# Four loads under way instead of eight in a fused three-block kernel

## The chip, the cores and the metric

The kernel runs on one core of a Trainium2 chip. The metric is the device time of one execution in microseconds (us). All times below come from the runs and from one profiled execution of the kernel.

## What is computed

Three blocks follow each other, all in float32, on 4 batches of 576 positions:

```python
def reference(**kwargs):
    attn_out = _attn_ref(q, k, v)              # (4, 8, 576, 64); heads 0-3 see 32 local keys, 4-7 see keys 32 apart
    x = attn_out.transpose(0, 2, 1, 3).reshape(B, S, H * D)
    x = _moe_ref(x, ...)                       # h = relu(x @ w_in); u * (w_spatial @ norm(v) + b_spatial) @ w_out
    return _moe2_ref(x, ...)                   # 4 experts: causal softmax attention, weighted by a top-2 gate
...
    scores = scale * np.matmul(q, k.transpose(0, 1, 3, 2))     # block 1
    scores = np.where(masks[None, :, :, :], scores, -1000000000.0)
    attn = np.exp(scores - scores.max(-1)); attn /= attn.sum(-1) + 1e-09
    return np.matmul(attn, v)
```

Inputs are q, k, v, and the weights of the two later blocks. Some weights arrive as float64 (`w_in`, `w_out`) and are split into two float32r halves on the chip, so that three matmuls stand for one float32 product (`mm3`, lines 618 to 620).

## The kernel before

**Order.** Nothing waits on a barrier between stages. Each piece of work is a generator (`a1_load`, `a1_scores`, `v_half`, `project`, ...) and a planner, `Plan.run`, picks from their steps one after the other by rank, by planned engine times, and by three tables of numbers (NUDGE, HOLD, LEAN). The order in which it picks is the order in which instructions stand on each engine: on PE, DVE, ACT and POOL, and on SP, which issues nearly all DMAs. Every engine works through its own row in order. Across engines, semaphores hold an instruction until its inputs are there.

**Loads.** All reads of inputs are issued by SP. Lines 796 and 799 load q and k of a pair of heads (288 KB each, `a1_load`), line 818 the values (`a1_load_v`, 48 to 256 KB a piece), line 666 a float64 weight (512 KB, `weight`), line 659 a float32 weight (144 to 288 KB), lines 733, 736 and 743 the tail of `w_spatial`. There are 100 of them, and they stand in places 1 to 100 of SP's row. Behind them on SP come only copies between tiles on the chip (L1362, L1366) and the stores of the result (L1622). The first 50 loads stand close together at the start; the next 50 wait for a buffer or for a stage to end and come in small bunches.

**What already holds a load back.** The framework gives each DMA one of eight semaphores in turn (DMAHW0 to DMAHW7), and a DMA that takes a semaphore again waits until the DMA that had it before has landed. So at most eight are under way.

**Steps that the prediction speaks of.** L1050 are the matmuls of block 1's attention with its values, on 64x64 corners of the array: short, and many. L981 and L983 turn the attention tiles (`a`, which POOL or DVE has just divided by its sums at L914). L844 and L856 are block 1's scores. L531 are matmuls on zeros, put in by `fill` where the planner sees PE idle in the first 46 us. L618 to L620 are dense products. On DVE, L673 is the first step on a float64 weight that has landed, L1062 subtracts the high half of block 1's result (which ACT copied at L639) from PSUM.

```python
        yield "sp", 0.46, [("a1", b)] + prev, dict(c=2)
        qt, kt = C([128, S], F, "q"), C([128, S], F, "k")
        nc.sync.dma_start(qt, qk[b, hp, :, 0, :])
```

Of the kernel before, what the change touches and what calls it, by code (L numbers as in the profile page):

```python
# [14 lines left out]
B, H, S, D = 4, 8, 576, 64  # L15
# [2 lines left out]
NEG = -8.0e9  # L18
NCHUNK = 75
EXPERTS_AHEAD = 4  # L20
TAILS = 3
ALONE = 3
TRANK = 15
# [444 lines left out]
def fused(tc, qk, vl, vw, vs, win, wsb, woutT, wp, wo, out):  # L468
    nc = tc.nc
# [6 lines left out]
    const, chunk, small, psum = [c.__enter__() for c in ctx]  # L476
    plan = Plan(dict(c=NCHUNK, w64=3, bd=TAILS, al=ALONE, eps=8, mx=8, ps=8, sq=PSUM_BANKS["d"] - 1, **PSUM_BANKS))
    plan.within = dict.fromkeys(PSUM_BANKS, "ps")
# [23 lines left out]
    def f(t):  # L502
        return t.bitcast(F)

    act, dve, pool, pe = nc.scalar, nc.vector, nc.gpsimd, nc.tensor


# [43 lines left out]
    m = mloc[:32]  # L551
# [13 lines left out]
    for h in range(2):  # L565
        for m, nr, off in ((mstr, 3, 0), (mstl, 2, 28)):
            m = m[64 * h:64 * h + 64].rearrange("p (c i) -> p c i", i=18)
# [7 lines left out]

    bd = [const.tile([128, 2, 128], R, name=f"bd{i}") for i in range(TAILS)]

# [74 lines left out]
    def weight(keys, src, r0, rows, c0, cols, after=(), summed=False, alone=False):  # L652


        n = len(keys)
        if src.dtype == F:
            yield "sp", 0.46, after, dict(c=1)
            m = C([rows, n * cols], F, "st")
            nc.sync.dma_start(m.rearrange("p (a c) -> p a c", a=n),
                              src[r0:r0 + n * rows, c0:c0 + cols].rearrange("(a p) c -> p a c", a=n))  # L660
            plan.dma(n * rows * cols * 4)
            plan.lat = 0.0
        else:
            yield "sp", 0.46, after, dict(w64=1)
            w = chunk.tile([rows, cols, 2], I32, name=nm("w64"), tag="w64", bufs=3)
            nc.sync.dma_start(w.rearrange("p a b -> p (a b)"),
                              src.bitcast(I32)[r0:r0 + rows, 2 * c0:2 * (c0 + cols)])
            plan.dma(rows * cols * 8)


            yield "dve", 1.75, (), dict(c=2)
            a, p2 = C([rows, cols], I32, "a"), C([rows, cols], I32, "p2")
            dve.tensor_scalar(a, w[:, :, 1], 3, 0x3FFFFFFF, op0=ALU.logical_shift_left, op1=ALU.bitwise_and)  # L673
            dve.scalar_tensor_tensor(a, w[:, :, 1], -0x40000000, a, op0=ALU.bitwise_and, op1=ALU.bitwise_or)
            dve.tensor_scalar(p2, a, -0x800000, None, op0=ALU.bitwise_and)
            if not summed:


                yield *(((("act", "dve"), (t_act(cols), t_fast(cols)))) if alone else hi_of(cols)), (), dict(c=2)
                hi, wl = (C([rows, cols], R, n) for n in ("wh", "wl"))  # L680
                if plan.eng == "act":
                    act.activation(hi, f(a), AF.Copy, scale=1 + 2.0 ** -22)
                else:
                    engine().tensor_scalar_mul(hi, f(a), 1 + 2.0 ** -22)
                yield "dve", 1.65, (), {}
                d = w[:, :, 1]
                dve.tensor_scalar(d, d, 23, None, op0=ALU.logical_shift_left)
                dve.scalar_tensor_tensor(f(a), w[:, :, 0].bitcast(dt.uint32), 2.0 ** -9, d, op0=ALU.mult, op1=ALU.add)
                dve.scalar_tensor_tensor(wl, f(a), 2.0 ** -43, f(p2), op0=ALU.mult, op1=ALU.mult)
                plan.give("w64")  # L690
                plan.give("c", 2)
                key, = keys
                W[key] = (hi, wl)
                plan.set(("W", key))
                return
            yield "dve", t_dve(cols), (), dict(c=1)
            m = C([rows, cols], R, "m")
            engine().scalar_tensor_tensor(m, w[:, :, 0].bitcast(dt.uint32), 2.0 ** -52, f(p2), op0=ALU.mult, op1=ALU.mult)
            plan.give("w64")
            yield *hi_of(cols), (), dict(c=1)  # L700
            hi = C([rows, cols], R, "wh")
            copy(hi, f(a))
            yield "pe", t_mm(cols, 6), (), dict(x=1)
            ps = P([rows, cols], "x")
            pe.matmul(ps, ident, f(a), start=True, stop=False)
            pe.matmul(ps, unit, m, start=False, stop=False)
            pe.matmul(ps, minus, hi, start=False, stop=True)
            plan.give("c", 3)
            yield *out_of(cols), (), dict(c=1)
            wl = C([rows, cols], R, "wl")  # L710
            copy(wl, ps)
            plan.give("x")
            key, = keys
            W[key] = (hi, wl)
            plan.set(("W", key))
            return
        yield *((("act", "dve"), (t_act(n * cols), t_fast(n * cols))) if alone else hi_of(n * cols)), (), dict(c=1)
        hi = C([rows, n * cols], R, "wh")
        copy(hi, m)
        yield *(("dve", t_dve(n * cols)) if alone else lo_of(n * cols)), (), dict(c=1)  # L720
        wl = C([rows, n * cols], R, "wl")
        engine().tensor_sub(wl, m, f(hi))
        plan.give("c")
        for i, key in enumerate(keys):
            W[key] = (hi[:, i * cols:i * cols + cols], wl[:, i * cols:i * cols + cols])
            plan.set(("W", key))

    def spatial_tail():

        n = S - 512  # L730
        yield "sp", 0.46, [("x",0,3,0)], dict(c=2)
        m, mb = C([128, S], F, "st"), C([97, S], F, "mb")
        nc.sync.dma_start(m[:n, :], wsb[512:S, :])
        plan.dma(n * S * 4)
        yield "sp", 0.46, (), {}
        nc.sync.dma_start(m[n:, :], wsb[512:S, :])
        plan.dma(n * S * 4)
        r = plan.ready
        yield "pool", 0.6, (), {}
        pool.memset(mb[64:97, :], 0.0)  # L740
        for row in (64, 96):
            yield "sp", 0.46, (), {}
            nc.sync.dma_start(mb[row:row + 1, :], wsb[S:S + 1, :])
            plan.dma(S * 4)
        plan.ready = max(plan.ready, r)
        yield *hi_of(S), (), dict(c=2)
        hi, wl = C([128, S], R, "wh"), C([97, S], R, "wl")
        copy(hi, m)
        yield *hi_of(S), (), {}
        copy(wl[64:97, :], mb[64:97, :])  # L750
        yield "dve", t_dve(2 * S, 2), (), {}
        dve.tensor_sub(wl[96:97, :], mb[96:97, :], f(wl)[96:97, :])
        dve.tensor_sub(wl[:n, :], m[:n, :], f(hi)[:n, :])
        plan.give("c", 2)
        W["sp", 4] = (hi, wl)
        plan.set(("W", ("sp", 4)))
# [31 lines left out]
    def a1_load(b, hp):  # L788
        local = hp < 2
        order = [(bb, h) for bb in range(B) for h in range(4)]  # L790
        n = order.index((b, hp))
        d = 4
        prev = [("a", *order[n - d], 1)] if n >= d else []
        yield "sp", 0.46, [("a1", b)] + prev, dict(c=2)
        qt, kt = C([128, S], F, "q"), C([128, S], F, "k")
        nc.sync.dma_start(qt, qk[b, hp, :, 0, :])
        plan.dma(128 * S * 4)
        yield "sp", 0.46, (), {}
        nc.sync.dma_start(kt, qk[b, hp, :, 1, :])
        plan.dma(128 * S * 4)  # L800
        r = plan.ready
        plan.set(("ld", b, hp))
        A1[b, hp] = dict(q=qt, k=kt, nk=64 if local else 54, v=[], a={}, x=None)
        plan.set(("qk", b, hp), r - plan.end)

    def a1_load_v(b, hp):
        local = hp < 2
        if wide(b, hp):
            parts = [(96, min(512, 1152 - i), vw[b - 2, hp, :, i:min(i + 512, 1152)]) for i in range(0, 1152, 512)]
        elif local:  # L810

            parts = [(128, 512, vl[b, hp, :, 512 * i:512 * i + 512]) for i in range(2)] + [(64, 256, vl[b, hp, :64, 1024:])]
        else:
            parts = [(128, 128 * (j1 - j0), vs[b, hp - 2, :, 128 * j0:128 * j1]) for j0, j1 in ((0, 2), (2, 6))]
        for i, (rows, cols, src) in enumerate(parts):
            yield "sp", 0.46, [] if i else [("ld", b, hp)], {} if i else dict(c=len(parts))
            t = C([rows, cols], F, "v")
            nc.sync.dma_start(t, src)
            plan.dma(rows * cols * 4)
            A1[b, hp]["v"].append(t)  # L820
        plan.set(("v1", b, hp), plan.ready - plan.end)
# [560 lines left out]
    def ahead(b, e):  # L1382
        n = 4 * b + e - EXPERTS_AHEAD
        return [("edone", *divmod(n, 4))] if n >= 0 else []
# [399 lines left out]
```

## Time and profile before

| | |
|---|---|
| median of 3 runs | 434.56 us (434.14 to 434.62) |
| the profiled execution | 434.02 us |
| its span, first to last instruction | 432.1 us |
| PE busy | 419.5 us, 97% of the span |
| DVE busy | 318.7 us, 74% |
| ACT busy | 267.1 us, 62% |
| POOL busy | 141.1 us, 33% |
| HBM read, written | 26.59 MB, 4.72 MB |

The page of the profile gives busy times, the DMA queues and the costliest groups. Further views of the same trace are used below: the waits (who waited for whom), the chain of work that ended last in order of time, a table by stretches of time, a timeline of one engine, and the DMA queues and issues of one stretch. "PEld" is the loading of PE's weights, which runs beside the matmuls. "Issue" as the cause of a wait means that the engine waited for nothing that the profile shows.

### The profile page before, as it was taken

What the parts mean: (1) busy time and instruction counts of PE and PEld (TensorE: products, weight loads), DVE (VectorE), ACT (ScalarE), POOL (GpSimd) and SP (SyncE); (2) the same over time, 40 slices, a digit from 0 to 9 for tenths busy, and PEclk for the clock granted to TensorE, in tenths of its full rate; (3) what the DMA queues carried; (4) which work ended last, traced back from release to release, by engine and by line L of the source; (5) the groups of instructions that cost most, each with busy time, mean ns of one, the idle gap of its engine ahead of it and who ended that gap; (6) DMA issues with size and microseconds to landing.
All of it is one profiled execution on the core that took longest, in us unless ns stands there. A gap on an engine that the chain in (4) does not pass through costs nothing.

```text
span 432.1 us, 11509 instructions
## 1 busy us (share of the span) xinstructions
PE 419.5 (97%) x4156; PEld 382.7 (89%) x4156; DVE 318.7 (74%) x1189; ACT 267.1 (62%) x827; POOL 141.1 (33%) x258
## 2 busy tenths in 40 slices
PE   7869999999999999999999999999999999999996
PEld 3557899999999889998999899999999999988885
DVE  6998998264577742347979863698888899988872
ACT  3666776154598841224405532887788779779973
POOL 3551876541152340221508911112022005215210
PEclk9999999999999999999999999999999999999999
DMA  7999105121561000334000006805251332162043
GB/s 297 340 361 308 35 2 175 67 79 36 157 205 44 2 2 2 122 101 167 2 1 2 2 0 155 194 1 126 67 134 43 94 79 58 24 160 98 26 148 121
DMA packets 22844, 43.58 MB, mean 101 GB/s; under 512 B 3202, under 2 KB 5634, under 8 KB 22788
## 3 DMA queue, kind: packets, MB, share of 16 engines
q1 hardware_dynamic: 22628, 42.72, 32.9%
q8 instruction: 33, 0.54, 0.5%
q14 instruction: 23, 0.19, 0.1%
q10 hardware_dynamic: 160, 0.13, 0.1%
HBM read 26.59 MB, written 4.72 MB: 72 GB/s over the span
## 4 chain that ended last, share of the span: by engine, by line
PE 95%; DVE 1%; DMA 1%; issue 1%; ACT 1%; POOL 0%; SPq 0%; ACTq 0%
PE pd L618 17%; PE pd L620 17%; PE pd L619 17%; PE pt L1488 4%; PE pd L1206 4%; PE pd L1207 4%; PE pd L1208 4%; PE px L1050 4%; PE ps L856 2%; PE px L1536 2%; PE ps L1401 2%; PE ps L1400 2%; PE px L1534 2%; PE px L1566 2%; PE pt L981 2%; PE pd L1210 1%
## 5 line engine op out<-in xcount | busy, mean ns | idle before, releaser
L1423 POOL TENSOR_SCALAR a<-a,asums 128x256 f32<-128x256 f32 (+3 forms) x23 | 23.1, 1010 | 87.1 <-DVE asums L1431 52.5
L914 POOL TENSOR_TENSOR a<-a,rs 128x216 f32<-128x216 f32 (+5 forms) x32 | 25.3, 797 | 55.2 <-DVE rs L912 26.3
L618 PE MATMUL pd<-xh,wh 128*128 128x288 f32 x128 | 38.8, 303 | 0.0
L1388 DVE CUSTOM_DVE_ANT_0 a<-ps,mqk 128x512 f32<-128x512 f32 (+4 forms) x72 | 33.5, 482 | 7.2 <-PE ps L1401 5.3
L1414 ACT ACTIVATE a<-a,amx 128x384 f32<-128x384 f32 (+3 forms) x64 | 35.6, 557 | 5.0 <-DVE amx L1388 4.9
L1206 PE MATMUL pd<-wh,vh 128*128 128x288 f32 x128 | 38.2, 298 | 0.0
L618 PE MATMUL pd<-gh,fh 128*128 128x288 f32 x128 | 38.1, 297 | 0.0
L619 PE MATMUL pd<-xl,wh 128*128 128x288 f32 x128 | 37.7, 295 | 0.0
L620 PE MATMUL pd<-gh,fl 128*128 128x288 f32 x128 | 37.7, 295 | 0.0
L1207 PE MATMUL pd<-wl,vh 128*128 128x288 f32 x128 | 37.7, 294 | 0.0
L620 PE MATMUL pd<-xh,wl 128*128 128x288 f32 x128 | 37.7, 294 | 0.0
L619 PE MATMUL pd<-gl,fh 128*128 128x288 f32 x128 | 37.7, 294 | 0.0
L1208 PE MATMUL pd<-wh,vlo 128*128 128x288 f32 x128 | 37.7, 294 | 0.0
L1121 DVE BATCH_NORM_STATS2 bst<-vr 128x6 f32<-128x512 f32 x18 | 12.4, 691 | 25.2 <-ACT vr L645 25.2
L1477 DVE TENSOR_TENSOR e<-pt,e 128x384 fp32r<-128x384 f32 (+1 forms) x48 | 27.6, 598 | 3.7 <-ACT e L639 3.2
L645 ACT ACTIVATE vr<-pd 128x512 f32<-128x512 f32 x17 | 10.1, 594 | 30.5 <-PE pd L620 29.0
L1214 DVE TENSOR_TENSOR u<-pd,u 128x288 f32<-128x288 f32 x32 | 13.9, 454 | 18.7 <-PE pd L1211 18.6
L1127 POOL TENSOR_TENSOR rstd<-rstd,neghalf 128x1 f32<-128x1 f32 x18 | 11.9, 664 | 47.4 <-DVE rstd L1125 38.7
L879 ACT ACTIVATE a<-a,mx 128x64 f32<-128x64 f32 (+1 forms) x72 | 24.9, 350 | 3.5 <-DVE mx L870 3.5
L618 PE MATMUL pd<-wh,xh 128*128 128x512 f32 x64 | 26.0, 406 | 0.0
L620 PE MATMUL pd<-wh,xl 128*128 128x512 f32 x64 | 25.1, 392 | 0.0
L619 PE MATMUL pd<-wl,xh 128*128 128x512 f32 x64 | 25.1, 392 | 0.0
(243 smaller groups left out, 1478.3 us busy)
## 6 DMA issues: line engine op xcount, KB each, us to landing
qk<-qk SPq DMA_DIRECT2D x64, 144.0 KB, 2.4
q<-in_qk_dram SPq DMA_DIRECT2D x16, 288.0 KB, 5.2
k<-in_qk_dram SPq DMA_DIRECT2D x16, 288.0 KB, 5.3
w<-in_win_dram SPq DMA_DIRECT2D x8, 512.0 KB, 6.3
out_dram<-o SPq DMA_DIRECT2D x16, 256.0 KB, 2.1
v<-in_vl_dram SPq DMA_DIRECT2D x8, 256.0 KB, 5.9
v<-in_vs_dram SPq DMA_DIRECT2D x8, 256.0 KB, 4.4
w<-in_woutT_dram SPq DMA_DIRECT2D x4, 512.0 KB, 4.4
```

The source lines that it names most:

```text
L618: pe.matmul(ps, ah, bh, start=i == 0, stop=False)
L619: pe.matmul(ps, ah, bl, start=False, stop=False)
L620: pe.matmul(ps, al, bh, start=False, stop=i == n - 1)
L879: act.activation(a[:, c], a[:, c], AF.Exp, bias=mx[:, c:c + 1], scale=-1.0, accum_out=sums[:, c, :1])
L914: engine().tensor_mul(x, x, rs[:, :n].unsqueeze(2).broadcast_to([128, n, nk]))
L1206: pe.matmul(ps, vh[:, fs], wh[:, c0:c0 + cn], start=(i == 0), stop=False)
L1207: pe.matmul(ps, vh[:, fs], wl[:, c0:c0 + cn], start=False, stop=False)
L1208: pe.matmul(ps, vlo[:, fs], wh[:, c0:c0 + cn], start=False, stop=False)
L1388: dve.tensor_tensor_reduce(a[:, s0:s0 + sn], ps, mask, op0=ALU.add, op1=ALU.min, scale=-0.125, scalar=m if s0 else 3.0e38, accum_out=m)
L1414: act.activation(a, a, AF.Exp, bias=m, scale=-1.0, accum_out=st["sums", e][:, i:i + 1])
L1423: engine().tensor_scalar_mul(a, a, r)
L1477: dve.tensor_sub(el, ps, f(eh))
```

## The change

Each load is issued through a small function `load`, which adds a dependency on the load four places ahead of it. The first four are free, and the second bound (200) is never reached by 100 loads.

```diff
+QUEUED = 4
+THROTTLED = 200
...
+    loads = []
+
+    def load(dst, src):
+        i = nc.sync.dma_start(dst, src)
+        if QUEUED <= len(loads) < THROTTLED:
+            tc.add_manual_dep(getattr(i, "ins", i), loads[-QUEUED].name,
+                              mybir.DependencyInfo(mybir.DependencyClass.Sync, mybir.DependencyReason.DATA),
+                              reason="few loads at a time")
+        loads.append(getattr(i, "ins", i))
...
-            nc.sync.dma_start(m.rearrange("p (a c) -> p a c", a=n),
+            load(m.rearrange("p (a c) -> p a c", a=n),
...
-            nc.sync.dma_start(w.rearrange("p a b -> p (a b)"),
+            load(w.rearrange("p a b -> p (a b)"),
...
-        nc.sync.dma_start(qt, qk[b, hp, :, 0, :])
+        load(qt, qk[b, hp, :, 0, :])
```

The other five loads (k, the values, the four of `spatial_tail`) are changed in the same way. The planner knows nothing of it: the rows of PE, DVE, ACT and POOL are the same instructions in the same order with the same waits, and SP has the same 202 instructions in the same order.

What differs is which semaphore a load waits for. SP's row of the kernel before at the start of the program (w is a float64 weight, q and k are a pair of heads, v their values):

```order
L666 DMA w645_159<-in_win_dram 128x1024
L666 DMA w646_161<-in_win_dram 128x1024
L796 DMA q7_163<-in_qk_dram 128x576
L799 DMA k8_164<-in_qk_dram 128x576
L796 DMA q9_167<-in_qk_dram 128x576
L799 DMA k10_168<-in_qk_dram 128x576 [waits DMAHW0_49]
L818 DMA v11_171<-in_vl_dram 128x512 [waits DMAHW1_49]
L818 DMA v12_173<-in_vl_dram 128x512 [waits DMAHW2_49]
```

Here the ninth load, k10, is the first that waits, for the first load (DMAHW0). The same places of SP in the changed kernel:

```order
L510 DMA w645_159<-in_win_dram 128x1024
L510 DMA w646_161<-in_win_dram 128x1024 [waits DMAHW0_49]
L510 DMA q7_163<-in_qk_dram 128x576 [waits DMAHW1_49]
L510 DMA k8_164<-in_qk_dram 128x576 [waits DMAHW2_49]
L510 DMA q9_167<-in_qk_dram 128x576 [waits DMAHW3_49]
L510 DMA k10_168<-in_qk_dram 128x576 [waits DMAHW4_49]
L510 DMA v11_171<-in_vl_dram 128x512 [waits DMAHW5_49]
L510 DMA v12_173<-in_vl_dram 128x512 [waits DMAHW6_49]
```

Now the fifth load waits for the first, and each later one for the load four places ahead: no instruction is added, each wait names a semaphore four places nearer.

## Rows read from the trace of the kernel before

**Rows 1.** The page: span, busy time by engine, the DMA queues (packets, MB, share).

```profile
span 432.1 us, 11509 instructions
...
PE 419.5 (97%) x4156; PEld 382.7 (89%) x4156; DVE 318.7 (74%) x1189; ACT 267.1 (62%) x827; POOL 141.1 (33%) x258
...
q8 instruction: 33, 0.54, 0.5%
```

**Rows 2.** Waits of PE, whole run: us in total, times, longest us.

```profile
PE px L1050 <- issue: 2.6, 2, 1.9
PE ps L844 <- DMA k<-in_qk_dram: 2.0, 1, 2.0
...
PE pt L981 <- issue: 1.4, 1, 1.4
```

**Rows 3.** The chain that ended last, 16 to 40 us: start us, us, what.

```profile
22.88 1.92 issue
...
28.91 1.36 issue
...
36.27 0.72 issue
```

**Rows 4.** By stretches: us, busy (count) of PE, PEld, DVE, ACT, POOL, clock, DMA, GB/s.

```profile
19.40:24.79 5.39, 3.48 (x126) 3.12 (x126) 5.25 (x34) 3.68 (x10) 3.27 (x6) 1.00 1.02 378
24.79:30.26 5.47, 4.11 (x125) 3.08 (x125) 4.75 (x14) 2.86 (x10) 2.29 (x7) 1.00 1.02 361
30.26:36.99 6.73, 6.00 (x127) 4.47 (x127) 6.20 (x13) 2.67 (x6) 1.88 (x5) 1.00 0.88 306
36.99:47.07 10.08, 10.07 (x124) 7.60 (x127) 8.94 (x53) 8.30 (x35) 5.65 (x15) 1.00 0.72 226
```

**Rows 5.** DMA queues in 0.1 us from 22.4, 27.7 and 47.9 us.

```profile
q8 instruction: 1, 0.02, 50.0%
...
q8 instruction: 1, 0.02, 70.3%
...
q8 instruction: 1, 0.02, 75.4%
```

**Rows 6.** DMA issues near 30.5, 74 and 113 us: KB each, us to landing.

```profile
w<-in_win_dram SPq DMA_DIRECT2D x1, 512.0 KB, 7.1
...
k<-in_qk_dram SPq DMA_DIRECT2D x1, 288.0 KB, 4.2
...
k<-in_qk_dram SPq DMA_DIRECT2D x1, 288.0 KB, 2.8
```

**Rows 7.** Timelines of POOL and PE: start us, us, engine line op [idle before].

```profile
27.61 0.82 POOL L914 TENSOR_TENSOR a<-a,rs 128x378 f32<-128x378 f32 x1 [3.76 <-DVE rs L912]
...
28.58 0.32 PE L981 MATMUL pt<-ident,a 128*118 128x128 f32 x1
...
63.28 1.33 POOL L914 TENSOR_TENSOR a<-a,rs 128x216 f32<-128x216 f32 x2 [0.51 <-DVE rs L909]
...
64.55 0.55 PE L981 MATMUL pt<-ident,a 128*118 128x128 f32 x3
```

**Rows 8.** Timeline of DVE: the same columns.

```profile
26.66 0.49 DVE L1062 TENSOR_TENSOR xl<-px,xh 128x320 fp32r<-128x320 f32 x1 [0.59 <-ACT xh L639]
...
37.78 0.64 DVE L1062 TENSOR_TENSOR xl<-px,xh 128x108 fp32r<-128x108 f32 x2 [1.16 <-ACT xh L639]
...
40.95 0.41 DVE L673 TENSOR_SCALAR a<-w 128x512 int32<-128x512 int32 x1
```

**Rows 9.** Waits of DVE from 8.8 to 73.2 us: total, times, longest.

```profile
DVE xl L1062 <- ACT xh L639: 1.7, 2, 1.2
```

**Rows 10.** By stage, columns as in rows 4.

```profile
22.90:37.00 14.10, 10.11 (x253) 7.55 (x253) 12.80 (x30) 6.98 (x20) 5.11 (x13) 1.00 0.96 340
37.00:73.20 36.20, 36.20 (x570) 31.77 (x570) 34.19 (x149) 28.72 (x101) 24.76 (x38) 1.00 0.31 95
73.20:174.00 100.80, 100.80 (x1194) 92.35 (x1193) 54.80 (x290) 55.72 (x236) 34.38 (x62) 1.00 0.24 72
```

More of the change, by code (lines that the diff above doesn't have):

```diff
@@ L732, in spatial_tail @@
         m, mb = C([128, S], F, "st"), C([97, S], F, "mb")
-        nc.sync.dma_start(m[:n, :], wsb[512:S, :])
+        load(m[:n, :], wsb[512:S, :])
         plan.dma(n * S * 4)
         yield "sp", 0.46, (), {}
-        nc.sync.dma_start(m[n:, :], wsb[512:S, :])
+        load(m[n:, :], wsb[512:S, :])
         plan.dma(n * S * 4)
@@ L742, in spatial_tail @@
             yield "sp", 0.46, (), {}
-            nc.sync.dma_start(mb[row:row + 1, :], wsb[S:S + 1, :])
+            load(mb[row:row + 1, :], wsb[S:S + 1, :])
             plan.dma(S * 4)
@@ L795, in a1_load @@
         qt, kt = C([128, S], F, "q"), C([128, S], F, "k")
-        nc.sync.dma_start(qt, qk[b, hp, :, 0, :])
+        load(qt, qk[b, hp, :, 0, :])
         plan.dma(128 * S * 4)
         yield "sp", 0.46, (), {}
-        nc.sync.dma_start(kt, qk[b, hp, :, 1, :])
+        load(kt, qk[b, hp, :, 1, :])
         plan.dma(128 * S * 4)
@@ L817, in a1_load_v @@
             t = C([rows, cols], F, "v")
-            nc.sync.dma_start(t, src)
+            load(t, src)
             plan.dma(rows * cols * 4)
```

## The prediction

> **What bounds the kernel now.** I read the page first: PE is busy 419.5 of 432.1 us [rows 1], so the end can only move if PE's idle time changes, or if something makes PE wait. The waits of PE say where that idle time lies. Two of the lines shown have no cause in the kernel at all: 2.6 and 1.4 us, 4.0 in three waits, are put down to "issue" [rows 2]. The one wait for a load is the first of all, 2.0 us for the first k; nothing that the change touches stands ahead of it. After that no load ever ends a wait of PE.
>
> The chain in order of time places the three: 1.92 us from 22.88, 1.36 from 28.91, 0.72 from 36.27 [rows 3]. All lie in the first 46 us, when the loads run. The table by stretches shows what they are. From the end of one wait to the end of the next PE has executed 125 to 127 matmuls and as many weight loads [rows 4], so about 256 instructions; and queue q8, named "instruction", moved 33 packets of together 0.54 MB [rows 1], 16 KB each, which is 8312 PE instructions in pieces of about 252. So PE stands still at the border of a piece of program that has not come yet. A packet of that queue begins at 22.4 and one at 27.7 us [rows 5], each 2.4 to 2.6 us before PE goes on (24.80, 30.27).
>
> How long does such a fetch take? PE crosses a border at 19.4, at 24.80 and at 30.27 (the starts of the stretches in rows 4), and the next piece's packet begins at 22.4 and 27.7: **3.0 and 2.9 us after the border**. After the border at 47.07, when the loads are done, it begins at 47.9: **0.8 us after** [rows 4, 5]. So about 2.1 us of each early fetch are spent waiting while the loads have the DMA engines (DMA share 1.02 in both stretches, rows 4). A load waits there too: one issued near 30.5 lands after 7.1 us, one issued into empty queues after 2.8 [rows 6].
>
> **The change, part by part.** No instruction is added or moved on any engine; 96 waits on SP now name a load four places back, where 92 named one eight back. Behind a waiting load stand only other loads: the 100 loads fill SP's first places, so copies and stores are not held.
>
> *Fetches.* With three other loads ahead of it, a load finds little queued. Four loads of 288 KB at the observed rates (about 350 GB/s, rows 4, 10) take 3.4 us, of which 2.8 is the time of one load alone; so about 0.5 us of waiting is left, where 7.1 less some 3.4 (a 512 KB load alone, my estimate from 2.8 plus 224 KB at 350 GB/s) leave 3.7 now. If a fetch's wait shrinks like a load's, it falls from 2.1 to 0.3 us; bounds are 0 (the row at 47.9) and 2.1 (unchanged). I take 0.5. A fetch from border to execution is then 0.8 + 0.5 + 2.5 = 3.8 us, against 5.4, 5.5 and 6.7 now. PE's own work in the three pieces is 3.48, 4.11 and 6.00 us [rows 4]. What remains of the waits is 0.3, 0 and 0: **3.7 of 4.0 us leave PE's idle time.**
>
> The Trainium skill says, in "Runtime: NRT & Kernel Launch", section "Instruction fetch mechanics", that instructions come in blocks of 16 KiB over a queue of the sequencer's own and that crossing a border is mostly hidden. The trace agrees on the blocks (256 instructions apart) and not on the hiding: three borders cost 4.0 us. By the page there would be nothing to gain here, and the time would stay at 434.6 us.
>
> *What is late next.* PE gets earlier only as far as its inputs do. The first 1.6 us are mostly lost at once: the transpose at 28.58 reads a tile that POOL ends at 27.61 + 0.82 = 28.43 [rows 7], and POOL waited for DVE. DVE in turn had stood still 0.59 us before 26.66 for ACT's copy of PE's late result [rows 8]; only that comes back. So PE gains 0.59 + 0.15 = 0.7 there, then the whole second wait (its fetch now starts earlier and the border comes no earlier than 28.2) and the third: 0.7 + 1.36 + 0.72 = 2.8 us at 37.
>
> From there DVE decides. Between 8.8 and 73.2 us the waits of DVE over 0.3 us are two, 1.7 us together, both for ACT's copy behind a late PE result [rows 9]: 0.59 and 1.16 [rows 8]. Otherwise it works through, 34.19 of 36.20 us in the stage from 37 on [rows 10]. So it can get 1.75 us ahead and no more until 73. PE reads DVE's and POOL's tiles with little in hand: the transposes from 64.55 to 65.10 read tiles of which POOL ends the last at 63.28 + 1.33 = 64.61, some 0.2 us before its use [rows 7]. So of the 2.8 us about **1.75 + 0.2 = 1.95** are left at 65. After 73 PE is busy without a gap (100.80 of 100.80, rows 10) and the other engines have time to spare, so the 1.95 us stay to the end.
>
> *The loads themselves.* A load can only come later. Alone it lands 2.8 us after its issue, so four under way could carry 4 x 288 KB in 2.8 us, 420 GB/s, more than the 340 to 378 that flow now [rows 4, 10]; in a bunch of six with four under way, one took 4.2 [rows 6], which would be 280 GB/s. I take about 3.2 us (370 GB/s), nearer the first row, since loads now start one by one as others land, and not in a burst as there. Then the stream is as fast as now, or up to 1 us late at 37. Nothing waits for it: the weight issued near 30.5 lands by 38.0 and DVE comes to it at 40.95 [rows 6, 8], 2.9 us later, or 1.2 with DVE 1.75 us ahead. Later loads come into queues that are a quarter used (DMA share 0.24, rows 10). Cost: zero, covered by that margin; if it is gone, DVE waits.
>
> *Sum.* On the profiled execution: 434.0 - 1.95 = 432.1. Its median of runs is 0.5 higher, so **432.6 us**; with the fetch wait between 0 and 1 us and the loss to DVE between nothing and 0.8, 431.8 to 433.5.
>
> **The rivals.**
>
> *A part of it, 433.9.* The fetch's wait falls only to 1.5 us (T = 4.8). The first border is passed at 24.2, the second at 29.0, 1.3 us earlier than now, and the third wait goes; of that DVE passes on about half, or late loads eat it: 0.3 to 1.1 us gained, 433.5 to 434.3.
>
> *No change, 434.6.* The fetch does not wait behind the queue of loads but for its turn on a busy engine. The load queue is never empty with four under way either, so the turn comes as late as now: the three waits stay at 1.92, 1.36 and 0.72, and loads come early enough, 434.3 to 434.9. For it: the fetch's extra 2.1 us is less than a load's extra 3.7. Against it: the extra 2.1 us are more than twice what a whole load takes of the engines (288 KB at 350 GB/s, 0.8 us), so it is more than one turn. The Trainium skill has this rule in "DMA: Bandwidth & Descriptors", section "Queues, rings and completion order": each DMA engine takes turns between queues, a packet at a time. The trace speaks against it as the only delay, by the 2.9 to 3.0 us from border to packet, but no run here shows the turns.
>
> *Slower, 438.* Four under way don't fill the DMA engines: at 280 GB/s (the 4.2 us row) what now flows from 8.8 to 37 us (28.2 us at some 350 GB/s, 9.9 MB) takes 35.3 us, 7.1 more. The weight issued near 30.5 then lands near 45 at the latest, where DVE wanted it at 40.95, and DVE stands up to 4 us; it has no gap to take that back before 73, and PE has some 0.2 us in hand [rows 7], so the end comes 3 to 3.9 us later, 437.6 to 438.5, even with the fetches repaired. It decides from about 3 us of delay (38.0 to 40.95), a rate under 9.9 MB / 31.2 us = 317 GB/s.
>
> **How the numbers follow.** A measurement of this kernel tells 0.2%, 0.9 us, from no change. Chances: the forecast 0.62, a part of it 0.14, no change 0.14, slower 0.10. The range leaves out the slower case and the far ends: 431.7 to 434.9. Faster by over 0.2% (under 433.7): the forecast and half of the part, 0.68; within 0.2%: the rest of the part, no change and a little of the slower case, 0.22; slower by over 0.2%: 0.10. The likeliest case's own range is 431.8 to 433.5.
>
> **What would show it.** In the profile after, the "issue" waits of PE should be at most 0.5 us in total, with instruction packets beginning within 1.5 us of each border. A 288 KB load should land some 3 us after issue in the first 40 us (now up to 7). DVE's two waits for ACT's copy should be gone, and a new wait of PE for POOL or DVE should stand near 28 us, another between 41 and 65. Wrong would be: "issue" waits of the same length (no change), a DVE wait for a weight load near 40 us or GB/s under 317 in the first stretches (slower), or PE gaining more than 2.3 us (then DVE was not the limit until 73).

## The result and the profile after

The changed kernel takes **440.57 us** (median, 438.30 to 441.15) beside 434.35 us of the kernel before on the same chip: a ratio of 1.0136, 95% interval 1.0097 to 1.0175. It is slower by 6.2 us, outside the predicted range. The profiled execution is the shortest of its runs, 438.3 us with a span of 436.5 us, 4.4 us more than the span before [rows 1]. One execution of a kernel below (444.19 us, without weights to wait for) was in a slower state of the chip and is left out. The new lines shift the numbering: L1050 of before is L1062 here, L981 is L993, L914 is L926, L673 is L685, L639 is L651, and all loads of the change stand at L510.

The waits of PE, whole run (us in total, times, longest), beside [rows 2]:

```profile
PE pt L993 <- POOL a L926: 3.2, 3, 2.0
PE px L1062 <- ACT aT L651: 2.3, 1, 2.3
...
PE px L1062 <- DVE xl L1074: 1.1, 1, 1.1
PE ps L868 <- DVE rs L924: 0.7, 1, 0.7
```

The three "issue" waits, 4.0 us before, are gone altogether; the forecast had 3.7 of them go. In their place PE waits for POOL, ACT and DVE. What those waited for stands in the waits of DVE (8.8 to 73.2 us, beside [rows 9]) and in two lines of those of ACT (37 to 60 us):

```profile
DVE a L685 <- DMA w<-in_win_dram: 6.9, 4, 3.2
```

```profile
ACT wh L694 <- DVE a L686: 2.4, 1, 2.4
ACT wh L651 <- DMA st<-in_wsb_dram: 1.4, 1, 1.4
```

So both engines end up waiting for loads. DVE stands 6.9 us for float64 weights (w), where it stood for none in this stretch before. ACT stands 1.4 us for a float32 weight (st). The page's chain of work that ended last has PE for 87% of the span and DMA for 6%; before it was 95% and 1%:

```profile
PE 87%; DMA 6%; DVE 5%; ACT 1%; issue 0%; DVEq 0%; SPq 0%
```

In order of time (start, length, what) it runs through four loads between 16 and 62 us:

```profile
19.40 4.99 DMA w<-in_win_dram
...
28.93 5.38 DMA w<-in_win_dram
...
42.51 4.21 DMA k<-in_qk_dram
...
46.78 5.30 DMA st<-in_wsb_dram
...
52.10 0.68 ACT wh L651
52.78 0.28 ACT aT L651
...
53.11 1.30 PE px L1062 x70
```

The last rows are worth following. ACT's row of work has "wh" (a conversion of the weight st) right ahead of "aT", the copy that PE's products at 53.11 need. The weight lands at 52.08, so ACT stands, and PE stands 2.30 us behind it. Before, the same conversion began at 47.59 and did not wait, because its weight had landed at 43.09.

The table by stages shows the stream of loads itself (time, busy and count of PE, PEld, DVE, ACT, POOL, granted clock, DMA share, GB/s), beside [rows 10]:

```profile
8.80:22.90 14.10, 12.88 (x296) 8.41 (x295) 13.72 (x104) 10.52 (x48) 7.03 (x17) 0.93 0.86 266
22.90:37.00 14.10, 11.01 (x242) 8.22 (x236) 10.31 (x25) 6.53 (x20) 4.55 (x12) 0.88 0.82 259
37.00:48.00 11.00, 10.33 (x155) 7.83 (x150) 7.56 (x46) 7.23 (x33) 3.11 (x8) 1.00 0.83 256
48.00:60.00 12.00, 9.70 (x177) 8.54 (x166) 11.32 (x54) 8.81 (x32) 9.93 (x19) 0.86 0.52 155
```

It moves 259 GB/s from 22.9 to 37 us, where 340 flowed before [rows 10]. A single load is faster than it was (the weights of 512 KB in the chain land after 4.99 and 5.38 us, where one needed 7.1 [rows 6]), but too few are under way. From 37 to 60 us the loads are still coming; before, the first 50 were done at 46.3 us. DVE's busy time from 22.9 to 37 falls from 12.80 to 10.31 us.

The sum of the change on the page: PE is busy 422.1 us (419.5 before), and idle for 14.4 (12.6 before):

```profile
PE 422.1 (97%) x4156; PEld 384.6 (88%) x4156; DVE 317.5 (73%) x1189; ACT 267.2 (61%) x827; POOL 140.9 (32%) x258
```

The idle time is 4.0 us less in instruction waits and some 5.8 more in others. The busy time grows where the granted clock falls to half, 1.2 instead of 2.4 GHz. It does so after two of PE's new waits, of 1.98 us from 26.24 and 2.30 us from 50.81 (and once earlier in this execution, from 7.4 to 10.8 us, mostly over matmuls of zeros; the scores behind them begin at 11.54 us, in the kernel before at 11.72):

```profile
28.20:31.20 3.00, 2.98 (x10) 2.54 (x11) 2.93 (x6) 0.73 (x2) 2.60 (x8) 0.50 0.75 217
55.20:58.60 3.40, 3.40 (x15) 3.08 (x13) 3.30 (x10) 3.10 (x14) 1.96 (x4) 0.50 0.09 31
```

Not every wait of about that length is followed by half clock: in the kernel before, 1.92 us at 22.88 was not [rows 3, 4].

What each part costs can be read from the times at which PE comes to the same instructions. Two groups of the same work, before and then after (start, length, what):

```profile
50.11 1.30 PE L1050 MATMUL px<-aT,v 64*64 64x32 f32 x70
...
60.02 1.35 PE L1050 MATMUL px<-aT,v 64*64 64x32 f32 x72
```

```profile
53.11 1.30 PE L1062 MATMUL px<-aT,v 64*64 64x32 f32 x70 [2.30 <-ACT aT L651]
...
64.54 1.35 PE L1062 MATMUL px<-aT,v 64*64 64x32 f32 x72
```

At the border behind which the first instruction wait stood (24.80 before, 22.17 now) PE is 2.6 us ahead of the kernel before, and at 40.05 still 0.26. At 42.20, behind a wait for DVE, it is 0.57 late, and at 53.11, behind the wait for "aT", 3.00. From there it waits for nothing, but at 64.54 it is 4.52 late: the difference comes with the stretch at half clock, 55.2 to 58.6, and stays (4.49 at PE's last matmul). So of the 4.4 us in this execution some 3.0 are what the waits behind late loads cost beyond what the fetches gave, and 1.5 are the clock's. The median is 2 us above this execution, and no trace says where those stand.

This leaves four questions. What do four loads carry, and why less than I took? Is it the weights that cost, or any load? Can the loss by the clock be taken away? And was the gain, the instruction waits, worth what the forecast said?

### The profile page after: what moved, and what is told of

Same layout as the page of the kernel before. It is cut to its first block, busy times and chain, and to the rows that moved or that the text cites. A ratio compares the mean times of both kernels' runs of the same rounds, so it can differ in the third digit from the quotient of the medians.

```text
span 436.5 us, 11508 instructions
## 1 busy us (share of the span) xinstructions
PE 422.1 (97%) x4156; PEld 384.6 (88%) x4156; DVE 317.5 (73%) x1189; ACT 267.2 (61%) x827; POOL 140.9 (32%) x258
## 3 DMA queue, kind: packets, MB, share of 16 engines
HBM read 26.59 MB, written 4.72 MB: 72 GB/s over the span
## 4 chain that ended last, share of the span: by engine, by line
PE 87%; DMA 6%; DVE 5%; ACT 1%; issue 0%; DVEq 0%; SPq 0%
PE pd L630 16%; PE pd L631 16%; PE pd L632 16%; PE pt L1500 4%; PE pd L1218 4%; PE pd L1219 4%; PE pd L1220 4%; DMA w<-in_win_dram 3%; PE px L1062 3%; PE px L1548 2%; PE ps L1413 2%; PE ps L1412 2%; PE px L1546 2%; PE ps L868 2%; PE px L1578 2%; DMA st<-in_wsb_dram 1%
## 5 line engine op out<-in xcount | busy, mean ns | idle before, releaser
L926 POOL TENSOR_TENSOR a<-a,rs 128x216 f32<-128x216 f32 (+5 forms) x32 | 25.4, 798 | 58.8 <-DVE rs L924 30.4
```

The lines of the kernel that those rows point to most:

```text
L926: engine().tensor_mul(x, x, rs[:, :n].unsqueeze(2).broadcast_to([128, n, nk]))
```

## Experiments: how much a number of loads carries

**Loads alone, pieces of 288 KB.** No work but loads; each phase starts when the one before has landed.

```python
PHASES = [(1, 8, 0), (2, 16, 0), (3, 24, 0), (4, 24, 0), (5, 24, 0), (6, 24, 0), (8, 24, 0), (4, 24, 1), (8, 24, 1)]  # under way, loads, matmuls beside
...
            for k in range(n):
...
                i = nc.sync.dma_start(t, qk[k // 8, (k // 2) % 4, :, k % 2, :])
...
                for back in (range(1, 9) if k == 0 else (depth,) if k >= depth else ()):
                    if back <= len(loads):
                        tc.add_manual_dep(i, loads[-back].name, info(), reason="few loads at a time")
```

> This kernel computes nothing of the reference: it only loads 288 KB blocks of q and k, in groups with 1, 2, 3, 4, 5, 6 and 8 loads under way, then with 4 and with 8 while PE works through 500 short matmuls, and stores zeros. Theory A (a load's own way is long, about 4 us once others are under way, and four do not fill the engines): with four, 288 KB land every 0.95 us or slower (310 GB/s or less) also without any PE work, with eight every 0.71 us. Theory B (four fill the engines, but each instruction fetch or other traffic holds up one of the 16 engines, and with four under way the next load waits for that slowest one): four alone reach 390 GB/s or more, within 5% of eight, and only the group beside PE falls to about 300.

Measured, in the steady part of the phases with 2, 3, 4, 5, 6 and 8 under way, then four beside short matmuls (columns: time, PE, PEld, DVE, POOL, clock, DMA share, GB/s):

```profile
30.00:44.00 14.00, 0.00 (x0) 0.00 (x0) 0.00 (x0) 0.00 (x0) 1.00 0.68 210
54.00:72.70 18.70, 0.00 (x0) 0.00 (x0) 0.00 (x0) 0.00 (x0) 1.00 0.82 260
82.00:96.90 14.90, 0.00 (x0) 0.00 (x0) 0.00 (x0) 0.00 (x0) 1.00 0.92 307
108.00:120.70 12.70, 0.00 (x0) 0.00 (x0) 0.00 (x0) 0.00 (x0) 1.00 0.96 326
131.00:141.60 10.60, 0.00 (x0) 0.00 (x0) 0.00 (x0) 0.00 (x0) 1.00 1.01 379
153.00:161.70 8.70, 0.00 (x0) 0.00 (x0) 0.00 (x0) 0.00 (x0) 1.00 1.04 393
177.00:189.30 12.30, 12.30 (x236) 12.30 (x234) 0.00 (x0) 0.00 (x0) 1.00 0.91 299
```

A single load lands after 2.6 to 2.9 us here as well, and with one under way a load comes every 2.76 us, 107 GB/s. Two carry nearly twice that, but four carry 307 and not four times 107: with four under way each takes 3.2 to 4.4 us. The matmuls take little (299). The first theory of the expectation holds (310 GB/s or less with four, without any other work), the second does not. So even the best case of four, one size and no other work, lies under the 317 GB/s from which my slower rival was to decide.

**Loads alone, the kernel's own sizes.** The kernel's first 44 loads in its order, 12.85 MB in pieces of 64 to 512 KB, four times over.

```python
PHASES = [(4, 44, 0), (8, 44, 0), (4, 44, 1), (8, 44, 1)]
...
name, row, col, rows, cols = LOADS[k]
...
i = nc.sync.dma_start(t[:rows, :cols], src[row:row + rows, col:col + cols])
```

> Loads alone: the kernel's own first 44 loads (12.85 MB in pieces of 64, 128, 256, 288 and 512 KB, in the kernel's order) four times over, each pass starting when the one before has landed: with four under way, with eight, and both again beside 200 short matmuls on TensorE. Pieces of 288 KB gave 315 GB/s with four under way and 391 with eight. The mixed sizes are what makes it 255 GB/s in the kernel (a wait on a large piece holds back the small ones behind it): the first pass takes 48 to 51 us, the second 33 to 37. The kernel's engines are what makes it 255: 40 to 43 us and 33 us alone, and longer beside the matmuls.

Measured for the first three passes, then for the middle of the first two (same columns):

```profile
0.73:47.57 46.84, 0.00 (x0) 0.00 (x0) 0.48 (x1) 0.00 (x0) 1.00 0.84 274
47.65:86.02 38.37, 0.00 (x0) 0.00 (x0) 0.00 (x0) 0.00 (x0) 1.00 0.95 335
86.10:135.65 49.55, 21.54 (x400) 21.41 (x400) 0.00 (x0) 0.00 (x0) 1.00 0.81 260
...
3.00:45.00 42.00, 0.00 (x0) 0.00 (x0) 0.00 (x0) 0.00 (x0) 1.00 0.87 281
50.00:84.00 34.00, 0.00 (x0) 0.00 (x0) 0.00 (x0) 0.00 (x0) 1.00 1.02 362
```

Four under way take 46.8 us (274 GB/s) without any other work and 49.6 (260) beside matmuls; the kernel has 256 to 266. Eight take 38.4 us (335) and 39.4 beside matmuls; the kernel before had 340 to 353. Both expectations missed the first pass, 46.8, by a little (it lies nearer to the one that blames the sizes), and the second, 38.4, which was to take 33 to 37. A whole pass holds its slow start and end, so it is the middle that stands beside the 307 above: 281, and 271 beside matmuls. So the larger part of the way from 307 to the kernel's 256 to 266 is the mixture of pieces, some 10 are the matmuls, and a small rest is not explained. Why the mixture costs was not tested. That a place in a queue of four says nothing of bytes can be a part of it at most, for eight lose by the mixture as well: 362 in the middle, where equal pieces had 393.

## Experiments: how many, and where

**Five, six and seven.**

```diff
-QUEUED = 4
+QUEUED = 5      # 6 and 7 in the other two
```

> The change with five loads under way. Late weights as the cause: between four and six, 433.5 to 438, DVE's waits for weights 1 to 4 us where four had 6.9, PE's waits for instructions under 1 us in total. Rival (any wait on an earlier load costs): 439 to 441 as with four.

> The change with six loads under way. Theory A or B alike (the loss is that weights come late to DVE): a 288 KB load lands about 5 us after issue, the loads flow at 320 GB/s or more, DVE waits less than 1.5 us for weights between 20 and 50 us, and the time falls to 432.5 to 435. Rival (the waits as such cost on SP, or PE's clock falls whatever the depth): the time stays above 437.

> The change with seven loads under way. Late weights as the cause: as with eight within 0.3%, 433.5 to 435, with the three waits of PE for instructions still there for the larger part (2.5 to 4 us in total). Rival (any wait on an earlier load costs): above 437.

| under way | us, median | ratio, 95% interval | PE "issue" from 8.8 us, us | DVE for w, us | first st lands at |
|---|---|---|---|---|---|
| 8 (before) | 434.49 | 1 | 4.0 | 0 | 43.09 |
| 7 | 433.07 | 0.9974 (0.9947 to 1.0) | 1.9 | 0 | 43.35 |
| 6 | 433.48 | 0.9986 (0.9962 to 1.001) | 1.4 | 0 | 44.66 |
| 5 | 435.31 | 1.0039 (1.0011 to 1.0066) | 0 | 4.2 | 50.03 |
| 4 | 440.57 | 1.0136 (1.0097 to 1.0175) | 0 | 6.9 | 52.08 |

(The medians are of each kernel's runs, the last three columns of its profiled execution.) The waits on SP as such cost nothing that could be told: six and seven have them too, and neither is told from no change. Five is slower, and the lateness of the loads goes with it. With five, DVE stands for a weight; with six it does not:

```profile
DVE a L685 <- DMA w<-in_win_dram: 4.2, 3, 3.7
```

(For five, 1 to 4 us had been expected there; for seven, 2.5 to 4 us of instruction waits.) The instruction waits shrink as the queue does, with six to:

```profile
PE px L1062 <- issue: 1.1, 2, 0.9
PE pt L993 <- issue: 0.3, 1, 0.3
```

**Four, from the 21st load on.**

```diff
-        if QUEUED <= len(loads) < THROTTLED:
+        if 20 <= len(loads) < THROTTLED:
```

> The limit of four holds from the 21st load on alone; the first 20 go out as before. Late weights: the weight load that landed at 45.2 us (37.6 before) was 5 us late already at load 22 and lost another 2.5 us after; here only the last part is lost, it lands at 40 to 41 us, about when VectorE wants it (40.95 us), and the second and third instruction wait (2.1 us) go, so 432 to 433.5. If the rate of four loads costs more wherever it stands (loads land late by the amount of the whole deficit), 436 or more.

Measured: 435.47 us, ratio 1.0025 (1.0000 to 1.0050), between the two expectations. The weight landed at 41.24, close to what was expected, and DVE waited only 0.5 us for weights, but the first st still came at 49.93 and PE stood 0.7 us for "aT" near 50 us. The first instruction wait (2.3 us) stayed and the other two went:

```profile
PE px L1062 <- issue: 2.3, 1, 2.3
PE pt L993 <- POOL a L926: 1.6, 2, 1.0
PE px L1062 <- ACT aT L651: 0.7, 1, 0.7
```

I had looked at one load only, the weight; the st behind it was 6.8 us late.

**Bytes instead of loads.** A load waits until at most 1.5 MB are under way with it.

```diff
-QUEUED = 4
+QUEUED = 1500000
...
+        sizes.append(4 * int(np.prod(dst.shape)))
+        back = next((k for k in range(1, len(sizes)) if sum(sizes[-k - 1:]) > QUEUED), 0)
-        if QUEUED <= len(loads) < THROTTLED:
-            tc.add_manual_dep(getattr(i, "ins", i), loads[-QUEUED].name,
+        if back and len(loads) < THROTTLED:
+            tc.add_manual_dep(getattr(i, "ins", i), loads[-back].name,
```

> The limit counts bytes instead of loads: a load waits until no more than 1.5 MB are under way with it (five pieces of 288 KB, or three of 512). If an instruction packet waits for the bytes ahead of it and the engines need some 1.4 MB under way, this keeps the stream at 340 GB/s or more with packets 2 us or less after the border, and gives 431.5 to 433. If bytes are no better a measure than the count, it is like five or six loads, 433.5 to 435.3.

Measured: 437.9 us, ratio 1.0067 (1.0039 to 1.0095), a miss: worse than five loads. The stream fell to 265 GB/s from 22.9 to 37 us, DVE waited 5.3 us for weights, and one instruction wait of 1.0 us was left. With bytes counted, the loads go out in the same order and each still waits for one before it. The expectation was wrong in its count: three pieces of 512 KB are 1.57 MB, so that only two are let through at a time, and one with three of 288 KB. For such pieces the limit is four or less, and not five.

**Seven once more**, beside the one above:

> Seven loads under way, measured again beside the others of this job: 433.07 us at a ratio of 0.9974 the first time. A real gain repeats at 0.996 to 0.999; if it was scatter, the ratio is 0.999 to 1.002.

Measured: 433.61 us, ratio 0.9983 (0.9955 to 1.0011). Both measurements of seven lie under 1 by about what can be told from no change; together they point to 0.2%, but neither interval excludes no change. It is the best version found that computes all, and a gain is not established.

## Experiments: which loads, the clock, and what the waits were worth

**No weight to wait for.** All twelve w pieces are loaded as before, but DVE reads a small tile instead of all but the first of them; those weights are zero. (The expectations say the last five. But the test counts the loads issued when DVE's step is placed, and the trace has eleven first steps that read the small tile and one that reads w.)

```diff
+    there = const.tile([128, 32, 2], I32, name="there")
+    dve.memset(there, 0)
...
+            late = len(loads) > 15
...
+            w0, w1 = ((there[:rows, :, j].unsqueeze(1).broadcast_to([rows, cols // 32, 32]) if late else w[:, :, j])
+                      for j in range(2))
```

> The changed kernel (each load waits on the load four places ahead), except that VectorE's conversions of the last five 512 KB weight pieces read a small tile that is there from the start; the five pieces are still loaded, but nobody waits for them (so those weights are zero and the output is not the reference's). Late weights: VectorE's 6.9 us of waits for weights were the price and the three instruction waits of TensorE (4.0 us) were a real gain, so this kernel comes out 3 to 4 us below the kernel before, 430.5 to 431.5, without any TensorE wait marked issue over 0.5 us. The slower stream as such: q, k and v come late as well and hold TensorE up, so at least 437. Waits for something else of the same size: 433 to 436.

> The control to the one before: the same small tile in place of the last five weight pieces, but the waits reach back eight loads, which is no limit here. Late weights: in the kernel before VectorE does not wait for a weight, so nothing changes, 434.0 to 434.9, and TensorE stands about 4 us in waits marked issue. If the small tile itself (shorter reads, zero weights) makes the kernel faster, it shows here: 432 or less, and then the first kernel has to be read against this one.

Measured: 437.3, 438.75 and 443.26 us with four (ratio 1.0112, 1.0053 to 1.0171), and a median of 434.85 with eight (1.0010, 0.9978 to 1.0042). The small tile costs nothing, as the control says. With it DVE no longer waits for a weight, and **no gain can be told** from the 1.0136 of the changed kernel: the theory that the late weights alone are the price, which gave 430.5 to 431.5, falls. The waits of PE with four (from 8.8 us), and the loads on its chain:

```profile
PE ps L874 <- DMA k<-in_qk_dram: 3.5, 1, 3.5
PE pt L999 <- POOL a L932: 2.3, 3, 1.1
PE px L1068 <- ACT aT L653: 1.5, 1, 1.5
```

```profile
38.10 3.19 DMA k<-in_qk_dram
...
47.28 6.06 DMA st<-in_wsb_dram
```

PE is now ready for k before k has landed, and stands 3.5 us; then ACT waits for st until 53.34, 1.3 us later than in the changed kernel. Weights, k, v and st stand in one queue, and all of it is late. Who meets the lateness first only gives it a name.

**Filling the waits.** 18 matmuls of zeros ahead of the two longest waits of PE, to see whether the clock is a loss of its own.

```diff
+            for _ in range(8 * ((b, hp, g) == (0, 3, 1))):
+                pe.matmul(pt, zeros[:, :rows], zeros.unsqueeze(1).broadcast_to([128, k, 128]), start=True, stop=True)
...
+        for _ in range(10 * ((b, hp) == (1, 0))):
+            pe.matmul(px[0], zeros, zeros.unsqueeze(1).broadcast_to([128, 4, 128]), start=True, stop=True)
```

> The changed kernel with 18 matmuls of zeros put where TensorE stood longest, 8 (1.7 us) ahead of the transposes at 28.2 us and 10 (2.2 us) ahead of the products at 53.1 us, into the tiles that are written next. The clock as a part of the loss: TensorE's granted clock stays 1.00 in 28 to 32 and 55 to 59 us, where it was at half before, and the time falls by 1.3 to 2.6 us, to 438.0 to 439.3. Not on the path: TensorE only waits longer behind (for VectorE's weights), and the time stays 440 to 441.

Measured: 440.46 us, ratio 1.0133 (1.0099 to 1.0168), as without them. The filling did not keep the clock up in the profiled execution, which is the slowest of the six (443.22 us): PE stood 1.70 us for an instruction packet, behind the first two of the zeros, and 1.90 us for "aT" again, behind the other zeros, and went on at about half clock:

```profile
29.10:32.80 3.70, 3.70 (x12) 2.43 (x13) 2.64 (x6) 0.12 (x1) 3.19 (x10) 0.54 0.56 176
...
56.60:62.60 6.00, 6.00 (x124) 5.61 (x120) 5.76 (x17) 5.09 (x23) 4.50 (x6) 0.50 0.28 96
```

So its verdict on the clock is not a clean one. But another of its runs had a mean granted clock of 1.000 and a span of 438.1 us, 6 us above the span of before. So full clock alone does not bring the time back. How large the clock's part is that run can't say: it left no trace of its waits, and it has 18 matmuls more.

**Fewer bytes.** Nine of the twelve w pieces are not loaded at all, with four and with eight under way: the last five of the eight among the first 50 loads (2.6 MB less in the early queue, as the expectations have it), and the four of w_out, which came from 175 us on, where PE had no gap before. HBM reads fall from 26.59 to 21.87 MB. DVE reads the small tile as above.

```diff
+            if len(loads) < 15:
+                load(w.rearrange("p a b -> p (a b)"), ...)
```

> Four loads under way, and the last five 512 KB weight pieces are not loaded at all (VectorE reads the small tile as before, so those weights are zero and the output is not the reference's): 2.6 MB less ahead of 45 us, about 10 us of the queue at 255 GB/s. The rate of the stream is what costs with four, and the instruction waits are a real gain: now nothing comes late and 3 to 4 us stay gained, 430.5 to 431.7. If a short queue costs in another way (its waits, the landing times of single loads), or if TensorE's instruction waits were no loss, 434 or more.

> The control to the kernel with four loads under way and five weight pieces left out (431.68 us): the same five pieces are not loaded, but the waits reach back eight loads, which is no limit here (the weights are zero and the output is not the reference's). The limit of four made the gain: here the queue is as deep as before while it lasts, TensorE still stands 3 to 4 us in waits marked issue, and the time is 434 to 435. The 2.6 MB less made the gain: the queue runs dry early, instruction packets come soon, and the time is 431 to 432.5, so that the limit of four has shown no gain of its own. Both in part: 432.5 to 434.

Measured: 431.68 us with four (ratio 0.9942, 0.9919 to 0.9964) and 431.95 with eight (0.9932, 0.9901 to 0.9964). With four, PE, DVE and ACT wait for no load between 8.8 and 73.2 us, at 261 and 239 GB/s, and the kernel is 2.9 us faster than before. By itself this looks like the forecast gain. The control takes it away from the limit: with eight it is the same. The "issue" waits with eight and then with four, from 8.8 us:

```profile
PE pt L1000 <- issue: 0.9, 1, 0.9
PE px L1069 <- issue: 0.5, 1, 0.5
```

```profile
PE px L1069 <- issue: 0.8, 1, 0.8
```

Leaving the pieces out cuts the instruction waits from 4.0 to 1.4 us, and the span falls by 2.4 us (432.1 to 429.7). That looks as if an instruction wait taken away were worth nearly its length. But six loads under way leave the same 1.4 us, and their median is only 1.0 us under the kernel before, at most 1.7 by its interval. So either six loses something elsewhere or the missing bytes gain something else, and what such a wait is worth stays open between the two. The limit of four takes away 0.6 us more, and no gain of it can be seen between the two times.

## Why the prediction was wrong, point by point

- **Fetches: right in the waits, half right in the delay.** The waits put down to "issue" went from 4.0 us to none; 3.7 was forecast. PE crosses borders of 256 instructions at 18.93 and 22.17 us, and instruction packets start at 19.6 and 23.4, 0.7 and 1.3 us after; it was 3.0 and 2.9 before [rows 4, 5]. But it crosses the borders that lay at 37.00 and 47.07 before at 36.91 and 47.71, and their packets start at 39.4 and 50.5, 2.5 and 2.8 us after, where the prediction wanted 1.5 at most. Two stretches from border to border, as in [rows 4], and the two late packets, as in [rows 5]:

```profile
18.93:22.17 3.24, 3.24 (x127) 2.93 (x126) 3.14 (x27) 2.04 (x6) 2.06 (x5) 1.00 0.81 231
36.91:47.71 10.80, 10.13 (x142) 7.63 (x138) 7.36 (x42) 6.94 (x31) 2.82 (x7) 1.00 0.83 255
```

```profile
q8 instruction: 1, 0.02, 60.1%
...
q8 instruction: 1, 0.02, 74.8%
```

No wait comes of the late ones because PE is 10.8 and 6.7 us on the way to its next border. So one fetch with four loads under way is not always short. Nor was it 2.9 to 3.0 us throughout before: the packets for the borders at 30.27 and 37.00 started 3.8 and 6.5 us after them, and the prediction took only the two lower figures. The rival with the three waits unchanged is out. Its turns on a busy engine are not tested by four loads, since the engines were not busy all the time (DMA share 0.81 in the first stretch). Six loads speak against turns alone: from 8.8 to 37 us the share is 0.94 and 0.98, beside 1.00 and 0.96 before, and the waits fall to 1.4 us.
- **What an instruction wait is worth: not settled.** I let 1.95 of the 3.7 us reach the end, because of DVE. The kernel with the weight pieces left out loses 2.6 us of such waits and 2.4 us of span, the one with six loads under way the same waits and 1.0 us of its median. A limit by DVE at 1.95 is neither borne out nor excluded.
- **The loads: wrong, and this decided.** The failing step is "I take about 3.2 us (370 GB/s)" for four loads under way. The kernel moved 256 to 266 GB/s. I had two rows, 2.8 us for a load alone and 4.2 in a bunch of six, and took a value near the first because loads would start one by one. But with four under way, alone and of one size, they carried 307 GB/s, and 3.2 to 4.4 us was the time of each. The 4.2 us row was the nearer one. And its 280 GB/s was no lower bound either: the kernel's mixture carries 281 in its middle with nothing beside it, 271 beside matmuls, and the kernel less.
- **"Nothing waits for it": wrong.** I set the margin by one load, the weight that DVE took at 40.95. The stream is late as a whole, by 5.2 us at the 22nd load (27.55 instead of 22.35) and by 9 at the first st (52.08 instead of 43.09). DVE met it four times, and ACT met it at st, ahead of a copy for PE. Had that one margin held, others would have broken, as the run without weights to wait for shows.
- **The slower rival was the case, and too mild.** It gave 437.6 to 438.5 at 280 GB/s, by way of the same weight, with a chance of 0.10. Its mechanism is the one seen, though its place is any load and not that weight: the median comes out 2 us above its end, at a lower rate still and with a loss by the clock that it did not have. Its own condition, under 317 GB/s, would have deserved the weight of evidence that I gave to the row of a load alone.
- **The clock: not foreseen.** After two of PE's new waits the clock was at half. In the profiled execution the second of these stretches is 1.5 us of the 4.4; the first was taken up by later waits. For the median's 6.2 us the split stays open, and the one run at full clock was still 6 us slower.
- **A slip in the chances.** The forecast and half of the part make 0.69, not 0.68. Nothing hangs on it.

## What to carry to other kernels

A limit on the loads under way is a limit on their rate: take it from a row in which that many are under way and of the kernel's own sizes, never from the time of a load alone. Where a stream of loads is limited, ask for every consumer in the order of the queue how late it can bear its load, and not only for the nearest one; an engine that waits in order passes its wait on to whatever stands behind it. When a change takes away one cost and adds another, run a control in which only one of them can act: the kernel with weight pieces left out looked like the gain of the limit until the same was run without the limit. And look in the trace which instructions a control reached: the small tile was meant for five pieces and stood for eleven.

## What the runs showed of the hardware

- The rate rises with the number of 288 KB loads under way from 107 GB/s (one) by 210, 260, 307, 326 and 379 to 393 (eight). Four, which I had expected to be enough, reach 78% of that.
- When the pieces are of mixed sizes, the same engines carry 274 GB/s with four and 335 with eight over a whole pass, 281 and 362 in its middle.
- How long PE stands at borders of its program goes with the depth of the queue: 4.0 us in three waits with eight loads under way, 1.9 with seven (both times), 1.4 with six, none with five and four; with eight and 2.6 MB less in the early queue it is 1.4. The delay of a single instruction packet does not go with it as plainly: with four under way it was 0.7 and 1.3 us at two borders, 2.5 and 2.8 at two later ones.
- Half clock came after waits of PE of 1.98 and 2.30 us, and not after one of 1.92 us; 3.4 us of work at half clock put 1.5 us on the end of the execution.
- A conversion of a weight on ACT, with 4.5 us of margin before, became what PE waited for when its load came 9 us later.
